# Three engine programs as loop bodies that run once, and a down projection in 512-column products

## The chip, the cores and the metric

The kernel runs on one core of a Trainium2 chip. The time is device microseconds (us) of one execution. The span is the time from the first to the last instruction in the profile of one execution; the time of an execution is a little longer than its span, and both are given below.

## The reference

One decode step of a gated mix of an attention block and a gated feed-forward block, both on the same four rows `x` (4 x 512, bf16).

```python
g = sigmoid((x * gate_w).sum(-1, keepdims=True))
# a: 32 query heads over 8 key/value heads, the last W = 4096 of 16384 positions
q = (x @ wq)                       # 4 x 4096
p = softmax(q . k / sqrt(128))     # per head, over 4096 positions
a = (p . v) @ wo                   # wo is 4096 x 512
# b: gated feed-forward with a relu gate
gate, up = x @ W_gate, x @ W_up    # 512 x 1792 each
b = (gate * (gate > 0) * up) @ W_down     # W_down is 1792 x 512
return g * a + (1 - g) * b         # 4 x 512
```

The window of keys and values is 4 batches x 8 heads x 4096 positions x 128 values, 33.5 MB each in bf16; with the weights some 81 MB have to be read.

## The kernel before

The work is cut into eight sets `s` (`NSET`), each one batch and four of its eight key/value heads. For each set one 4 MB transfer brings the keys into `Ksb[:, s % 2]` (`load_k`, line 217) and one the values into `Vsb[:, s % 2]` (`load_v`, line 221). Both buffers are double; `load_k(s)` waits until the scores of set `s - 2` have been made, `load_v(s)` until the value products of set `s - 2` are done. All bulk transfers are issued by SyncE (SP) in one written order: `wq`, keys and values in turn, `W_gate`, `W_up` (into the key buffer), the last values, `W_down` (into the value buffer), and `wo` in five pieces at `WO_CUTS` (lines 235 to 244), of which the last two (`WOL`) are halves over columns. ScalarE (ACT) issues two small loads of `x` and `gate_w` first of all (lines 224 and 225).

For each set, TensorE (PE) transposes the keys in eight fills of eight 128 x 128 transposes (`kt`, line 352), VectorE (DVE) and ACT copy the fills back (lines 359 and 357), PE makes the scores in two pairs (`scores`, line 373), DVE adds a mask and takes the maximum (line 383), a small product and a DVE operation spread the maximum (lines 390 and 395), ACT takes the exponent (line 403), DVE transposes the probabilities (line 413), PE multiplies by the values (`values`, line 421) and ACT copies the result (line 430). The set's maximum, exponent and value products are written one set later than its scores.

A small class `Program` collects the operations of each engine in lists, with named events between them; `emit` writes an engine's list as straight code with semaphore waits. For PE alone the list is cut at `turn_edge` marks: a head, four turns of two sets each as one hardware loop (`Fori`, lines 130 to 134, with a drain and semaphore decrements at its end), and a tail written straight behind the loop (line 136). The programs of DVE, ACT, GpSimd (POOL) and SP have no loop.

The tail holds the last set's maximum, exponent and value products, `combine(0)` and `combine(1)` (lines 440 to 451: the quotient by the row sums, rearranged into `oq`), `gateup` (line 457: `x` with `W_gate` and `W_up`; ACT takes the relu, DVE the product, transposes it and scales it by `1 - g` into `hT`, line 470), and the output products (`product`, line 503). These add `W_down` and `wo` into one accumulator `AB` for two halves of 256 output columns: half `u` uses the PE columns from `32 * u` on (`tile_position`), so that its result lies in partitions `32 * u` to `32 * u + 3`. There are 28 products for `W_down` (14 row blocks x 2 halves) and 64 for `wo`. DVE and ACT copy one half each into `outr` (lines 517 and 518), SP stores it (line 539), all engines meet at the end of the block (line 534), and SP waits for the store (line 556).

Of the kernel before, what the change touches and what calls it, by code (L numbers as in the profile page):

```python
# [1 line left out]

# [4 lines left out]
BF16 = mybir.dt.bfloat16  # L7
ACTF = mybir.ActivationFunctionType
ALU = mybir.AluOpType
# [10 lines left out]
NSET = 8  # L20
NFT = FF // 128
# [12 lines left out]
class Program:  # L34
# [81 lines left out]
            out.append((name is not None, tuple(here)))  # L116
        return out

    def emit(self, engine, eng, sems):
        ops = self.ops[engine]  # L120
        if engine != "pe":
            self.emit_list(eng, sems, engine, ops, {}, {})
            return
        t = self.turns
        self.emit_list(eng, sems, engine, ops[:t[0]], {}, {})
        first = self.signature(ops[t[0]:t[1]], {})
        for k in range(1, len(t) - 1):
            shift = {s: k * n for s, n in self.lowered.items() if s not in self.shared}
            assert self.signature(ops[t[k]:t[k + 1]], shift) == first, k
        with eng.Fori(0, len(t) - 1):  # L130
            self.emit_list(eng, sems, engine, ops[t[0]:t[1]], {}, {})
            eng.drain()
            for s, n in self.lowered.items():
                eng.sem_inc(sems[s], -n)
        shift = {s: (len(t) - 1) * n for s, n in self.lowered.items() if s not in self.shared}
        self.emit_list(eng, sems, engine, ops[t[-1]:], shift, {})


def bass_gated_mix__sliding_block_cached__glu_gated_reglu__decode_kernel(
# [13 lines left out]
    with ExitStack() as ctx:  # L153
        def sb(name, shape, dt):
            return ctx.enter_context(nc.sbuf_tensor(name, shape, dt))
# [16 lines left out]
        xsb = sb("xsb", [5, 512], BF16)  # L172
# [3 lines left out]
        gsb = sb("gsb", [128, 8], FP32)  # L176
# [12 lines left out]
        hrelu = sb("hrelu", [128, FQ], FP32)  # L189
        hrow = sb("hrow", [128, FQ], FP32)  # L190
        hcol = sb("hcol", [128, FQ], FP32)
        hT = sb("hT", [128, NFT * 4], BF16)
        outr = sb("outr", [4, 512], BF16)
        TRT = ctx.enter_context(nc.psum_tensor("TRT", [128, 2048], FP32))
        SCT = ctx.enter_context(nc.psum_tensor("SCT", [128, 1024], FP32))
        OB = ctx.enter_context(nc.psum_tensor("OB", [128, 512], FP32))
# [5 lines left out]
        Wd = Vsb[:, 0, 0:NFT * 512].rearrange("p (i w) -> p i w", w=512)  # L202
# [3 lines left out]
        P = Program()  # L206
# [45 lines left out]
        P.op("pool", lambda e: e.memset(xw[:, :], 0.0), ("XW0",))  # L252
        P.op("pool", lambda e: e.memset(mx[:, 1, :], 0.0))
        P.op("pool", lambda e: e.memset(pT[:, 1, :], 0.0))
        P.op("pool", lambda e: e.memset(xT[:, :, :].rearrange("p t r -> p (t r)"), 0.0))
        P.op("pool", lambda e: e.memset(qW[:, :, :, :].rearrange("p s h w -> p (s h w)"), 0.0), ("QZ",))
        P.op("pool", lambda e: e.memset(m4[:, :], -NEG), ("M4Z",))
# [40 lines left out]
        for t in range(4):  # L298
            P.op("pe", lambda e, t=t: e.matmul(FB[:, 32:36], gwB[:, t * 128:(t + 1) * 128], xT[:, t, 0:4],
                                               start=(t == 0), stop=(t == 3)),  # L300
# [5 lines left out]
        for t in range(4):  # L306
            for half in range(2):
                for g in range(4):
# [3 lines left out]
                        start=(t == 0), stop=(t == 3), tile_position=(0, 32 * g)),  # L312
# [140 lines left out]
        def gateup():  # L453
            for t in range(4):
                for which, W in ((0, Wg), (1, Wu)):
                    for g in range(4):
                        P.op("pe", lambda e, which=which, W=W, t=t, g=g: e.matmul(
                            TRT[32 * g:32 * g + 32, 512 * which:512 * which + FQ], xT[:, t, :], W[:, t, FQ * g:FQ * g + FQ],
                            start=(t == 0), stop=(t == 3), tile_position=(0, 32 * g)),
                            ("GU", which) if (t == 3 and g == 3) else None,  # L460
                            [("WG",), ("WU",)] + fills[-NTR:])
            G0 = TRT[:, 0:FQ]
            G1 = TRT[:, 512:512 + FQ]
            P.op("act", lambda e: e.activation(hrelu[:, :], G0, ACTF.Relu),
                 ("H0",), [("GU", 0)])
            P.op("dve", lambda e: e.tensor_tensor(
                hrow[:, :].rearrange("p (i c) -> p c i", i=NFT), G1.rearrange("p (c i) -> p c i", i=NFT),
                hrelu[:, :].rearrange("p (c i) -> p c i", i=NFT), ALU.mult), ("H1",), [("H0",), ("GU", 1)])
            P.op("dve", lambda e: e.transpose(hcol[:, :], hrow[:, :]), ("H2",), [("H1",)])
            P.op("dve", lambda e: e.tensor_tensor(  # L470
                hT[:, :].rearrange("p (i b) -> p i b", b=4),
                hcol[:, :].rearrange("p (i b) -> p i b", b=32)[:, :, 0:4],
                gsb[:, 4:8].rearrange("p (o b) -> p o b", o=1).to_broadcast([128, NFT, 4]), ALU.mult),
                ("H",), [("H2",), ("G",)], sem="vd")


# [17 lines left out]
        turn(NSET - 1)  # L494
        combine(0)
        gateup()
        values(NSET - 1)
        combine(1)
        AB = SCT[:, 0:512]
        oq3 = oq[:, :].rearrange("p (b i) -> p b i", b=4)  # L500

        def product(stat, mov, u, start, stop, name, waits):
            P.op("pe", lambda e: e.matmul(AB[32 * u:32 * u + 4, 0:256], stat, mov[:, 256 * u:256 * u + 256],  # L503
                                          start=start, stop=stop, tile_position=(0, 32 * u)), name, waits)

        for i in range(NFT):
            for u in range(2):
                product(hT[:, 4 * i:4 * i + 4], Wd[:, i, :], u, i == 0, False, None,
                        [("WD",), ("H",), ("SCC", NSET - 1, 1)])
        for k in range(len(WO_CUTS) - 1):  # L510
            for i in range(WO_CUTS[k], WO_CUTS[k + 1]):
                for u in range(2):
                    product(oq3[:, :, i], Wo3[:, i, :], u, False, False, None, [("WO", k), ("OQ", 0), ("OQ", 1)])
        for u in range(2):
            for i in range(WO_CUTS[-1], 32):
                product(oq3[:, :, i], Wo3[:, i, :], u, False, i == 31, ("ACC", u) if i == 31 else None, [("WOL", u)])
        P.op("dve", lambda e: e.tensor_copy(outr[:, 0:256], AB[0:4, 0:256]), ("FIN", 0), [("ACC", 0)], sem="fin")
        P.op("act", lambda e: e.copy(outr[:, 256:512], AB[32:36, 0:256]), ("FIN", 1), [("ACC", 1)], sem="fin")  # L518

        per = {}  # L520
        for s, ev in (("vd", ("SCC", 1, 1)), ("va", ("OSB", 0))):
            after = ("SCC", 3, 1) if s == "vd" else ("OSB", 2)
            eng = {"vd": "dve", "va": "act"}[s]
# [8 lines left out]
        sems = {name: ctx.enter_context(nc.semaphore(name)) for name in names}  # L532
        nc.sync.dma_start(Vsb[:, 1, :], A_wq.rearrange("(p t) w -> p (t w)", p=128)).then_inc(sems["V1"], 16)  # L533
        with nc.Block() as block:
            @block.sync
            def _(e):
                P.emit("sp", e, sems)
                e.wait_ge(sems["fin"], 2)
                e.dma_start(out.rearrange("b o d -> (b o) d"), outr[:, :]).then_inc(sems["done"], 16)

            @block.gpsimd
            def _(e):
                P.emit("pool", e, sems)

            @block.tensor
            def _(e):
                P.emit("pe", e, sems)

            @block.vector
            def _(e):  # L550
                P.emit("dve", e, sems)

            @block.scalar
            def _(e):
                P.emit("act", e, sems)
        nc.sync.wait_ge(sems["done"], 16)


# [26 lines left out]
```

## Time and profile before

| | |
|---|---|
| three runs, median | 196.53 us (196.35 to 196.71) |
| profiled execution, its own time | 196.16 us |
| its span | 194.9 us |
| busy: PE, PE weight loads, DVE, ACT, POOL | 129.2, 101.0, 73.8, 66.5, 11.7 us |
| read from HBM | 81.01 MB, 416 GB/s over the span |

The busy times overlap: no engine is busy for more than two thirds of the span. PE and its weight loads (PEld) are one engine, and a matmul's end is modelled, so a busy PE is not PE at its peak. The rows "DMA queue, kind" give the packets of each queue, their bytes in MB, and the time that they took as a share of 16 DMA engines over the stretch that is asked for. Queue 1 carries what SP issues, queue 10 what ACT issues, and the kind "instruction" marks packets that carry instructions to the engines.

### The profile page before, as it was taken

To read this page: it belongs to the slowest core of one execution; us is meant where nothing else is said; L and a number is where in the kernel's file an instruction comes from. 1 tells how busy PE (TensorE), PEld (TensorE's weight loads), DVE (VectorE), ACT (ScalarE), POOL (GpSimd) and SP (SyncE) were. 2 spreads that over 40 slices of the span, in tenths; PEclk is the share of its full clock that TensorE was granted. 3 is DMA by queue.
4 is the path that set the end of the run, shared out by engine and by line. 5 is a ranking of instruction groups with operands and counts; after the bars stand their busy time and mean duration, and the time that the engine had idled before them with its cause. 6 is when DMAs were issued, how large, how long until landed. Compare 5 with 4: busy or idle time off the path is not lost.

```text
span 194.9 us, 3496 instructions
## 1 busy us (share of the span) xinstructions
PE 129.2 (66%) x1578; PEld 101.0 (52%) x1578; DVE 73.8 (38%) x95; ACT 66.5 (34%) x77; POOL 11.7 (6%) x43
## 2 busy tenths in 40 slices
PE   0137398788769649872887099649972987713964
PEld 0113396576556439651765097439651865503742
DVE  0200045259239323930682029324920492180000
ACT  2005025565255452435342424433435252510000
POOL 8820000000000000000000000000000000000000
PEclk9999999999999996999999859996999699995799
DMA  6999999999999999999999999999999999998992
GB/s 216 431 430 437 430 430 427 437 440 430 437 440 430 437 430 437 430 430 437 432 437 425 430 437 430 430 437 430 430 430 430 430 390 427 475 430 382 424 403 82
DMA packets 3881, 81.11 MB, mean 416 GB/s; under 512 B 409, under 2 KB 930, under 8 KB 1058
## 3 DMA queue, kind: packets, MB, share of 16 engines
q1 hardware_dynamic: 3864, 81.01, 97.3%
q8 instruction: 5, 0.08, 0.2%
q14 instruction: 2, 0.02, 0.0%
q10 hardware_dynamic: 10, 0.01, 0.0%
HBM read 81.01 MB, written 0.00 MB: 416 GB/s over the span
## 4 chain that ended last, share of the span: by engine, by line
DMA 59%; PE 21%; DVE 14%; ACT 3%; issue 1%; SPq 1%
DMA Ksb<-in_A_k_cache_dram 47%; PE TRT L352 15%; DMA Wbig<-in_A_wo_dram 12%; DVE Ksb L359 6%; DVE pT L413 5%; PE SCT L373 3%; DVE sc L383 3%; ACT Ksb L357 3%; PE OB L421 2%; PE SCT L503 1%; SPq L240 0%; PE FB L390 0%; SPq L533 0%; ACT outr L518 0%; SPq L235 0%
## 5 line engine op out<-in xcount | busy, mean ns | idle before, releaser
L352 PE MATMUL TRT<-identw,Ksb 128*128 128x128 f32 x512 | 75.1, 306 | 25.4 <-DMA Ksb<-in_A_k_cache_dram 17.5
L352 PEld LDWEIGHTS TRT<-identw,Ksb 128*128 128x128 f32 x512 | 65.9, 158 | 35.8 <-DMA Ksb<-in_A_k_cache_dram 18.8
L357 ACT COPY Ksb<-TRT 128x1024 f32<-128x1024 f32 x40 | 40.5, 1012 | 58.4 <-PE TRT L352 58.2
L359 DVE COPY Ksb<-TRT 128x1024 f32<-128x1024 f32 x24 | 29.4, 1223 | 40.1 <-PE TRT L352 40.1
L421 PE MATMUL OB<-Vsb,pT 128*32 128x256 bf16 x576 | 19.0, 288 | 7.5 <-DMA Vsb<-in_A_v_cache_dram 7.5
L373 PE MATMUL SCT<-Ksb,qS 128*32 128x512 bf16 x256 | 16.9, 381 | 8.8 <-ACT Ksb L357 8.8
L421 PEld LDWEIGHTS OB<-Vsb,pT 128*32 128x32 bf16 x576 | 16.4, 101 | 10.4 <-issue 7.9
L383 DVE CUSTOM_DVE_ANT_0 sc<-SCT,mask,mx 128x1024 bf16<-128x1024 f32 x8 | 10.3, 1284 | 26.9 <-PE SCT L373 26.9
L403 ACT ACTIVATE sc<-sc,negmax 128x2048 bf16<-128x2048 bf16 x8 | 16.0, 2002 | 10.7 <-DVE negmax L395 10.7
L413 DVE STREAM_TRANSPOSE pT<-sc 128x2048 bf16<-128x2048 bf16 x8 | 18.4, 2302 | 2.2 <-ACT sc L403 2.2
L430 ACT COPY osb<-OB 128x256 f32<-128x256 f32 x8 | 3.0, 372 | 31.1 <-PE OB L421 31.1
L373 PEld LDWEIGHTS SCT<-Ksb,qS 128*32 128x32 bf16 x256 | 5.2, 94 | 15.7 <-ACT Ksb L357 11.6
L383 DVE CUSTOM_DVE_ANT_0 sc<-SCT,mask 128x1024 bf16<-128x1024 f32 x8 | 9.8, 1225 | 2.2 <-PE SCT L373 2.2
L340 POOL COPY qS<-qW 128x64 bf16<-128x64 bf16 x8 | 1.8, 238 | 113.3 <-PE SCT L373 105.2
L390 PE MATMUL FB<-identw,mx 128*128 128x128 f32 x18 | 4.7, 343 | 5.7 <-issue 5.7
L395 DVE CUSTOM_DVE_ANT_0 mrow<-FB,qmask 128x128 f32<-128x128 f32 x8 | 2.3, 292 | 12.8 <-PE FB L390 12.8
L390 PEld LDWEIGHTS FB<-identw,mx 128*128 128x128 f32 x18 | 2.9, 200 | 7.6 <-issue 7.6
L292 PE MATMUL FB<-identw,xw 5*128 5x5 f32 x4 | 0.6, 262 | 8.5 <-POOL m L267 8.5
L503 PE MATMUL SCT<-Wbig,oq 128*4 128x256 bf16 x64 | 4.3, 273 | 2.6 <-DMA Wbig<-in_A_wo_dram 2.6
L310 PE MATMUL SCT<-Vsb,xT 128*32 128x512 bf16 x32 | 3.6, 631 | 2.8 <-DMA Vsb<-in_A_wq_dram 2.8
L292 PEld LDWEIGHTS FB<-identw,xw 5*128 5x128 f32 x4 | 0.6, 207 | 8.5 <-DVE xw L286 8.5
L503 PEld LDWEIGHTS SCT<-Wbig,oq 128*4 128x4 bf16 x64 | 2.7, 87 | 4.2 <-DMA Wbig<-in_A_wo_dram 3.6
(61 smaller groups left out, 42.7 us busy)
## 6 DMA issues: line engine op xcount, KB each, us to landing
Ksb<-in_A_k_cache_dram SPq DMA_DIRECT2D x8, 4096.0 KB, 24.2
Vsb<-in_A_v_cache_dram SPq DMA_DIRECT2D x8, 4096.0 KB, 32.2
Vsb<-in_A_wq_dram SPq DMA_DIRECT2D x1, 4096.0 KB, 12.3
Wbig<-in_A_wo_dram SPq DMA_DIRECT2D x1, 2048.0 KB, 21.5
Ksb<-in_B_W_gate_dram SPq DMA_DIRECT2D x1, 1792.0 KB, 19.7
Ksb<-in_B_W_up_dram SPq DMA_DIRECT2D x1, 1792.0 KB, 23.6
Vsb<-in_B_W_down_dram SPq DMA_DIRECT2D x1, 1792.0 KB, 17.0
Wbig<-in_A_wo_dram SPq DMA_DIRECT2D x1, 1280.0 KB, 24.1
```

What stands on the lines that cost most here:

```text
L310: P.op("pe", lambda e, half=half, t=t, g=g, col=col: e.matmul(SCT[32 * g:32 * g + 32, 512 * half:512 * half + 512], xT[:, t, :], Wq3[:, t, ...
L352: P.op("pe", lambda e, bk=bk, cc=cc, c=c: e.transpose(bk[:, cc * 128:(cc + 1) * 128], Kw[:, s % 2, c * 128:(c + 1) * 128], identw[:, :]), ...
L357: P.op("act", lambda e: e.copy(dst, bk), ("KTC", s, i), [("KT", s, i)], sem="va")
L359: P.op("dve", lambda e: e.tensor_copy(dst, bk), ("KTC", s, i), [("KT", s, i)], sem="vd")
L373: P.op("pe", lambda e, a=a, o=o, hb=hb, bank=bank: e.matmul(SCT[32 * a:32 * a + 32, 512 * hb:512 * hb + 512], qS[:, s % 2, o, :], k4[:, 16 ...
L383: P.op("dve", lambda e: e.tensor_tensor_reduce(sc[:, s % 2, pair * 1024:(pair + 1) * 1024], SCT[:, :], mask[:, :], 1.0, mx[:, s % 2, 0:1] ...
L390: P.op("pe", lambda e: e.matmul(FB[:, 384:512], mx[:, par, 1:2].to_broadcast([128, 128]), identw[:, :], start=True, stop=True), ("MT", s), ...
L403: P.op("act", lambda e: e.activation(sc[:, par, :], sc[:, par, :], ACTF.Exp, bias=negmax[:, par:par + 1], scale=SCALE, accum_out=rowsum[:, ...
L413: P.op("dve", lambda e: e.transpose(pT[:, par, :], sc[:, par, :]), ("PTT", s), [("EXP", s), ("PV", s - 2) if s >= 1 else None], sem="vd")
L421: P.op("pe", lambda e, g=g, blk=blk: e.matmul(OB[32 * g:32 * g + 32, 0:256], pT[:, par, 32 * blk:32 * blk + 32], Vsb[:, par, 256 * blk:256 ...
L430: P.op("act", lambda e: e.copy(osb[:, s, :], OB[:, 0:256]), ("OSB", s), [("PV", s)], sem="va")
L503: P.op("pe", lambda e: e.matmul(AB[32 * u:32 * u + 4, 0:256], stat, mov[:, 256 * u:256 * u + 256], start=start, stop=stop, tile_position=( ...
```

## The change

ACT's and DVE's whole programs and the tail of PE's program are each put into a block that ends in a compare-and-branch. A register is set to 0 ahead of the block, 1 is added at its end, and the branch back to the block's top is taken while the register is below 1, so never; the block runs once. At the block's top a branch hint is placed that names this branch (the compiled program marks it "likely taken"). PE's loop over the four turns is left as it is, and POOL and SP get no such block.

The products with `W_down` go over all 512 columns at once. Their stationary operand is widened to 36 columns, of which columns 0 to 3 and 32 to 35 hold the same four rows of `h` and the 28 between hold zeros; so 14 products write all 512 columns into both partition groups, where 28 wrote 256 columns each. `hT` grows from 56 to 504 columns for it, is zeroed once by POOL, and DVE's line that fills it writes two copies. The `wo` products of half 1 now write columns 256 to 511 of `AB`, where they wrote 0 to 255. The result is copied into `xsb`, which held `x`, instead of `outr`, which goes.

```diff
+    @contextmanager
+    def once(self, nc, engine, eng):
+        top, end = engine + "_once", engine + "_once_end"
+        reg = eng.alloc_register(engine + "_turns")
+        eng.reg_mov(reg, 0)
+        eng.br(top)
+        with nc.body(top, valid_engines=bass.OrderedEngineSet([eng.engine])):
+            place = eng.mark_branch_hint_location()
+            yield
+            eng.reg_add(reg, reg, 1)
+            eng.br_lt(reg, 1, on_true=top, on_false=end).branch_hint(place)
+        nc.switch_bb(end)
+
-    def emit(self, engine, eng, sems):
+    def emit(self, nc, engine, eng, sems):
         ops = self.ops[engine]
+        if engine in ("dve", "act"):
+            with self.once(nc, engine, eng):
+                self.emit_list(eng, sems, engine, ops, {}, {})
+            return
...
-        self.emit_list(eng, sems, engine, ops[t[-1]:], shift, {})
+        with self.once(nc, engine, eng):
+            self.emit_list(eng, sems, engine, ops[t[-1]:], shift, {})
...
-        hT = sb("hT", [128, NFT * 4], BF16)
-        outr = sb("outr", [4, 512], BF16)
+        hT = sb("hT", [128, 36 * NFT], BF16)
...
+        P.op("pool", lambda e: e.memset(hT[:, :], 0.0))
...
-                hT[:, :].rearrange("p (i b) -> p i b", b=4),
-                hcol[:, :].rearrange("p (i b) -> p i b", b=32)[:, :, 0:4],
-                gsb[:, 4:8].rearrange("p (o b) -> p o b", o=1).to_broadcast([128, NFT, 4]), ALU.mult),
+                hT[:, :].rearrange("p (k b i) -> p k i b", k=9, b=4)[:, 0:9:8],
+                hcol[:, :].rearrange("p (k i b) -> p k i b", k=1, b=32)[:, :, :, 0:4].to_broadcast([128, 2, NFT, 4]),
+                gsb[:, 4:8].rearrange("p (k o b) -> p k o b", k=1, o=1).to_broadcast([128, 2, NFT, 4]), ALU.mult),
...
+        def wide(stat, mov, start, waits):
+            P.op("pe", lambda e: e.matmul(AB[0:36, :], stat, mov, start=start, stop=False), None, waits)
...
-            P.op("pe", lambda e: e.matmul(AB[32 * u:32 * u + 4, 0:256], stat, mov[:, 256 * u:256 * u + 256],
+            P.op("pe", lambda e: e.matmul(AB[32 * u:32 * u + 4, 256 * u:256 * u + 256], stat, mov[:, 256 * u:256 * u + 256],
...
-            for u in range(2):
-                product(hT[:, 4 * i:4 * i + 4], Wd[:, i, :], u, i == 0, False, None,
-                        [("WD",), ("H",), ("SCC", NSET - 1, 1)])
+            wide(hT[:, i:i + 35 * NFT + 1:NFT], Wd[:, i, :], i == 0, [("WD",), ("H",), ("SCC", NSET - 1, 1)])
...
-        P.op("dve", lambda e: e.tensor_copy(outr[:, 0:256], AB[0:4, 0:256]), ("FIN", 0), [("ACC", 0)], sem="fin")
-        P.op("act", lambda e: e.copy(outr[:, 256:512], AB[32:36, 0:256]), ("FIN", 1), [("ACC", 1)], sem="fin")
+        P.op("dve", lambda e: e.tensor_copy(xsb[0:4, 0:256], AB[0:4, 0:256]), ("FIN", 0), [("ACC", 0)], sem="fin")
+        P.op("act", lambda e: e.copy(xsb[0:4, 256:512], AB[32:36, 256:512]), ("FIN", 1), [("ACC", 1)], sem="fin")
```

More of the change, by code (lines that the diff above doesn't have):

```diff
@@ L1 @@
-from contextlib import ExitStack
+from contextlib import ExitStack, contextmanager
 import concourse.bass as bass
@@ L536, in _ @@
             def _(e):
-                P.emit("sp", e, sems)
+                P.emit(nc, "sp", e, sems)
                 e.wait_ge(sems["fin"], 2)
-                e.dma_start(out.rearrange("b o d -> (b o) d"), outr[:, :]).then_inc(sems["done"], 16)
+                e.dma_start(out.rearrange("b o d -> (b o) d"), xsb[0:4, :]).then_inc(sems["done"], 16)
             @block.gpsimd
             def _(e):
-                P.emit("pool", e, sems)
+                P.emit(nc, "pool", e, sems)
             @block.tensor
             def _(e):
-                P.emit("pe", e, sems)
+                P.emit(nc, "pe", e, sems)
             @block.vector
             def _(e):
-                P.emit("dve", e, sems)
+                P.emit(nc, "dve", e, sems)
             @block.scalar
             def _(e):
-                P.emit("act", e, sems)
+                P.emit(nc, "act", e, sems)
         nc.sync.wait_ge(sems["done"], 16)
```

## Prediction

> **What bounds the kernel now.** I read the page's DMA queues first, then the end of the chain that ended last.
>
> ```profile
> span 194.9 us, 3496 instructions
> DMA  6999999999999999999999999999999999998992
> q1 hardware_dynamic: 3864, 81.01, 97.3%
> q8 instruction: 5, 0.08, 0.2%
> q14 instruction: 2, 0.02, 0.0%
> ...
> 166.62 24.15 DMA Wbig<-in_A_wo_dram
> ...
> 190.81 2.38 PE SCT L503 x32
> ...
> 193.22 0.36 ACT outr L518
> ```
>
> The DMA engines are busy in all slices but the first and the last two; SP's own queue takes 97.3% of them. The chain (start, length) ends in the transfer of `wo`, then the last products, one copy, and the store up to 194.9. So two things can move the end: the time at which the last of `wo` lands, and what follows it.
>
> Seven packets carry instructions. They use the same 16 engines as the data. Where they lie, by the DMA view over the stretches 31 to 32.5, 54 to 56, 93 to 95, 182 to 183.7 and 191.8 to 193 us, in this order:
>
> ```profile
> q8 instruction: 1, 0.02, 4.3%
> q8 instruction: 1, 0.02, 3.2%
> q14 instruction: 1, 0.01, 1.0%
> q8 instruction: 1, 0.02, 3.9%
> q8 instruction: 1, 0.02, 4.8%
> ```
>
> The two not shown are a q8 packet at 42 to 43.5 and a q14 packet at 104 to 105.5. Taking a packet as sent by one engine, its time is share x 16 x stretch: 0.043 x 16 x 1.5 = 1.03 us, then 1.02, 0.32, 1.06 and 0.92 us. Whose are they? The busy counts (PE, PEld, DVE, ACT, POOL in this order) between the first three q8 packets:
>
> ```profile
> 31.86:42.59 10.73, 8.61 (x129) 7.13 (x127) 4.97 (x8) 6.13 (x7) 0.24 (x1) 1.00 0.97 415
> 42.59:54.88 12.29, 9.13 (x138) 6.65 (x136) 7.07 (x7) 4.68 (x6) 0.24 (x1) 1.00 1.03 444
> ```
>
> PE runs 129 + 127 = 256 and 138 + 136 = 274 instructions; no other engine runs more than 8 or so. So q8 is PE's code, one packet for each 256 instructions or thereabouts: three in the first turn, none in turns 2 to 4 (the same code again), two in the tail. The two small ones, far apart, belong by exclusion to DVE and ACT, whose straight programs run in that time. The Trainium skill's page "Runtime: NRT & Kernel Launch", section "Instruction fetch mechanics", says that code comes in blocks of 16 KiB, 256 instructions, the next block while the current one runs; the q8 rows agree, the q14 rows have half blocks.
>
> What do these packets cost? The share of busy DMA engines (the last but one column) as the transfers run out:
>
> ```profile
> 190.40:190.80 0.40, 0.00 (x0) 0.00 (x0) 0.00 (x0) 0.00 (x0) 0.00 (x0) 1.00 0.77 254
> 190.80:191.20 0.40, 0.39 (x8) 0.33 (x10) 0.00 (x0) 0.00 (x0) 0.00 (x0) 1.00 0.42 151
> 191.20:191.50 0.30, 0.30 (x10) 0.24 (x8) 0.00 (x0) 0.00 (x0) 0.00 (x0) 1.00 0.36 123
> 191.50:191.90 0.40, 0.40 (x12) 0.24 (x6) 0.00 (x0) 0.00 (x0) 0.00 (x0) 1.00 0.29 86
> 191.90:192.10 0.20, 0.20 (x6) 0.03 (x4) 0.00 (x0) 0.00 (x0) 0.00 (x0) 1.00 0.54 156
> 192.10:192.40 0.30, 0.30 (x7) 0.24 (x8) 0.00 (x0) 0.00 (x0) 0.00 (x0) 1.00 0.12 34
> ```
>
> About seven engines (0.42 x 16) still work when the others are through, five after 191.5. They are late by up to 1.5 us, the length of one 16 KB packet and a little; five packets on a single engine would make one engine late by 5 us. So I read: each packet fell on an engine of its own, and the four 16 KB packets ahead of 191 us made four engines late by about the same. The work in these rows, 0.31 + 0.17 + 0.11 + 0.12 + 0.11 + 0.04 = 0.84 us of all 16, less 0.92 / 16 = 0.06 for the last packet, would end at 190.40 + 0.78 = 191.2 if spread evenly; it ends at some 192.4. So 1.2 us is all that no code at all could give.
>
> **The change part by part.** *Hints.* What a hint does no row here shows. At most, code is no longer brought from behind the branch: both q14 packets and the two in the tail go (four of seven). At least, nothing goes; below that, each hint brings its target again (three packets more). The three q8 packets of PE's first turn stay in every case, since that loop is untouched, and their three engines are late by as much as the fourth. The end of `wo` is the latest engine's, so removing the 182 us packet gives what it is later than the others: between 0 and its 1.06 us, and by the reading above nearly 0. The q14 packets (0.32 us) delay engines that are not the last: 0. The 191.9 us packet starts when at most five engines still carry data; unless it is on one of those (5 in 16, and then late by at most what data is left there), 0. Bounds of this edit: -1.2 and +1.06 us; I take 0, the row of six dwindling shares being the nearest.
>
> *Entry of the blocks.* A register move and a hint on each engine.
>
> ```profile
> PE FB L390 <- issue: 5.7, 4, 1.5
> 4.11 0.52 POOL L256 MEMSET qW<- 128x512 bf16 x1
> 8.00 0.44 DVE L286 COPY xw<-xsb 5x512 bf16<-5x512 bf16 x1 [8.00 <-POOL S L262]
> 9.79 0.16 DVE L297 COPY xT<-FB 128x16 bf16<-128x16 bf16 x1
> 13.12 3.60 PE L310 MATMUL SCT<-Vsb,xT 128*32 128x512 bf16 x32 [2.84 <-DMA Vsb<-in_A_wq_dram]
> 178.59 3.60 PE L421 MATMUL OB<-Vsb,pT 128*32 128x256 bf16 x64 [7.50 <-DMA Vsb<-in_A_v_cache_dram]
> ```
>
> PE's turn edge, with drain, six semaphore decrements, an addition and a branch, costs at most 1.5 us (first row: total, times, longest). An entry is bounded by 0 and that; I take 0.2, as it has two of nine instructions. On ACT it delays the loads of `x` and `gate_w`, behind which DVE's first operation, the transposes of `x` and the projection with `wq` are queued. `xT` is there at 9.95 and the projection waits for `wq` until 13.12: 3.2 us of cover. On PE, the wait for the last values (7.50 us) hides it. POOL's added memset (504 columns, so about the 0.52 us of `qW`'s 512) and DVE's second copy lie in the same two covers. All 0.
>
> *W_down.* 28 products over 256 columns, in pairs on two column groups, become 14 over 512 columns, unpaired.
>
> ```profile
> 184.62 1.69 PE L503 MATMUL SCT<-Vsb,hT 128*4 128x256 bf16 x28
> 187.70 1.92 PE L503 MATMUL SCT<-Wbig,oq 128*4 128x256 bf16 x32 [1.39 <-DMA Wbig<-in_A_wo_dram]
> 190.81 2.37 PE L503 MATMUL SCT<-Wbig,oq 128*4 128x256 bf16 x32 [1.19 <-DMA Wbig<-in_A_wo_dram]
> L373 PE MATMUL SCT<-Ksb,qS 128*32 128x512 bf16 x256 | 16.9, 381 | 8.8 <-ACT Ksb L357 8.8
> ```
>
> If pairs did not overlap before, nothing changes (1.69); if they did fully, twice 1.69 = 3.38. The score products (four 512-column ones side by side) give 16.9 / 64 = 0.264 per pass, 14 x 0.264 = 3.70. I take 3.38: the end moves from 186.31 to 188.00 (188.32 at 3.70). The first `wo` products then end at 189.92 (190.24) instead of 189.62, and the next piece of `wo` is awaited until 190.81. Cover left: 0.89 (0.57) us. Cost 0; at half the clock it would be 6.76 us, a rival below.
>
> *Exit.* An addition and a branch not taken, on three engines, then the meeting at the block's end.
>
> ```profile
> 192.93 0.41 DVE L517 CAST outr<-SCT 4x256 bf16<-4x256 f32 x1 [7.49 <-PE SCT L503]
> 193.60 0.35 SPq L539 DMA_DIRECT2D out_dram<-outr  x1
> SPq L556 <- DMA out_dram<-outr: 0.5, 1, 0.5
> ```
>
> PE ends at 193.18, DVE at 193.34, ACT at 193.58 by the chain; SP issues the store until 193.95 and after the meeting still waits 0.5 us for it. So PE may be late by 193.95 - 193.18 + 0.5 = 1.27 us, DVE by 1.11, ACT by 0.87. Two instructions, bounded by 0 and the turn edge's 1.5, taken at 0.2: hidden. The Trainium skill's page "Advanced Engine Details and Errata", section "Control Flow Timing", gives a compare-and-branch about 108 ns; by it the sum would be the same.
>
> Sum: 0 + 0 + 0 + 0. The span stays 194.9 and the profiled execution's 196.16 us with it. The median of the runs shown is 196.53, 0.37 above that execution; I forecast the median: **196.5 us**. About 0.2% (0.39 us) is what a measurement of this kernel can tell from no change.
>
> **The rivals.** *The exit stalls (slower).* If a hint sends the fetch back to the loop's top, the block behind the branch isn't there when the branch falls through. The last q8 packet was called near the end: after 191.9 only the 12 products of the rows from 192.07 on are left. The tail becomes 28 instructions shorter and some four longer, so PE's exit comes close to that very border. For it: the trace never shows a block running without a packet ahead of it. Against it: PE may read ahead while its products wait, and fetch early. Price: the store's issue to the end, 194.9 - 193.95 = 0.95 us for a small transfer, plus 0.92 for the packet: 1.87 us from 193.18 is 195.05, past the cover's end (193.95 + 0.5 = 194.45) by 0.60; for ACT with a half block 193.58 + 0.95 + 0.33 = 194.86, by 0.41. A second stall in what runs after the block would add 1.87. So +0.4 to +2.5, taken as +0.9: 197.4. It decides from a stall of 1.27 us on PE or 0.87 on ACT. The Runtime page's rule, in the section named, is that a branch outside the sequential stream waits for its block, and that straight code is to be preferred; by that rule the result is this rival.
>
> *The removed packet was the last (faster).* If the engine of the 182 us packet ends `wo` alone, or two packets share an engine in most executions, up to 1.06 us goes, and at most 1.2: 195.3 to 196.1, taken as 195.6. For it: packets are late in the right size. Against it: five engines, not one, are still busy after 191.5.
>
> *W_down at half clock (slower).*
>
> ```profile
> 37.15 1.92 PE L421 MATMUL OB<-Vsb,pT 128*32 128x256 bf16 x64
> ```
>
> The last set's 64 value products took 3.60 us where this earlier set's took 1.92, at half the clock. With `W_down` so: 184.62 + 6.76 = 191.4, then the 64 `wo` products, 1.92 + 2.37 = 4.3 us: 195.7 instead of 193.2, and 199.0 in all. Against it: the clock column (after POOL's) reads 1.00 from 190.4 on, and at 184.62 the products already run at the full pace of the rows above; it decides only if the half clock lasts longer than before.
>
> *The hint does nothing*: 196.5, part of the forecast.
>
> **How the numbers follow.** Forecast (with the idle hint) 0.47, its own range 196.1 to 196.9; exit stall or extra packets 0.31; half clock 0.02; removed packet 0.20. So faster 0.20, same 0.47, slower 0.33. The range reaches from 195.7 (a little beyond the middle of the faster case) to 197.9 (most of the stall).
>
> **What would show it.** Right: q8 packets at 31 to 56 us as before, none at 93 to 105, the shares after 190.8 unchanged, `W_down` ending before 188.4, the last product at 193.2. Wrong: PE's first product behind the wait for values later than 178.6; the last piece of `wo` landing over 0.4 us earlier or later; the wait of SP at the block's end longer than its wait for the store; a longer time with the same span, which would be a stall outside it.

## The result: 1.3% slower, by a stall of TensorE at its exit

| | before | changed |
|---|---|---|
| median | 196.44 us (196.14 to 196.71, 4 runs) | 199.02 us (4 runs) |
| ratio | | 1.0128, interval 1.0112 to 1.0144 |
| profiled execution | 196.16 us | 198.27 us |
| its span | 194.9 us | 196.6 us |
| beyond the span | 1.26 us | 1.67 us |

Of the four runs of the changed kernel three took 198.27, 198.88 and 199.16 us; the fourth, at 648.01 us, was disturbed by something that no record explains and is in the median, but not in the ratio. The profiled execution is the shortest of the three; the spans of the other two are 197.2 and 197.5 us, so more of the loss lies within the span there than in the views that follow.

The profiled execution is 2.1 us longer: 1.7 us within the span, 0.4 us beyond it. First the page's head and two of its queue rows, then the end of the timeline (start, length, engine, line; SPq and PEq stand for SyncE's and TensorE's instruction streams where they issue or wait; in the changed kernel `W_down`'s products are line 522, `wo`'s line 525, the store line 559):

```profile
span 196.6 us, 3481 instructions
...
q8 instruction: 4, 0.07, 0.1%
q14 instruction: 1, 0.01, 0.0%
```

```profile
167.54 0.48 PE L410 MATMUL FB<-identw,mx 128*128 128x128 f32 x2 [1.52 <-issue]
...
184.46 2.97 PE L522 MATMUL SCT<-Vsb,hT 128*36 128x512 bf16 x13
...
187.83 1.92 PE L525 MATMUL SCT<-Wbig,oq 128*4 128x256 bf16 x32 [0.41 <-DMA Wbig<-in_A_wo_dram]
...
191.02 2.28 PE L525 MATMUL SCT<-Wbig,oq 128*4 128x256 bf16 x32 [1.27 <-DMA Wbig<-in_A_wo_dram]
...
193.72 0.35 SPq L559 DMA_DIRECT2D out_dram<-xsb  x1
```

The `wo` products end at 193.30, 0.12 us later than before, and the store is issued 0.12 us later. Up to here that is all the loss. What follows is in the view of SP's own waits, one row of before and the one of the changed kernel for the same place, the meeting of the engines at the block's end:

```profile
SPq L534 <- PEq L534: 0.2, 1, 0.2
```

```profile
SPq L554 <- PEq L554: 2.2, 1, 2.2
```

SP now waits 2.2 us for PE, where it waited 0.2; and its wait for the store, 0.5 us before, is no longer in the view, since the store had long landed. That is the loss in the span: 2.0 more, 0.5 of it covered by the store, 0.12 from the later `wo`: 1.6 of the 1.7 us. In the trace's records PE's branch begins at 193.01 and the next instruction of its stream, the drain, at 196.30: 3.29 us, of which the last products fill the first 0.3.

The DMA view shows what moved in that time. There is no q8 packet from 176 to 190 us, where before had one at 182; there is one in the stretch 193.5 to 195.5:

```profile
q8 instruction: 1, 0.02, 2.8%
```

0.028 x 16 x 2 = 0.90 us of one engine: one 16 KB block of code, fetched while the 4 KB store of the result is all that moves besides. It starts at 193.96, 0.95 us after the branch, and PE goes on 1.45 us after it ended. That PE waits for this block is a reading so far; the experiments bear on it.

And the packets that the hints removed? The share of busy DMA engines (last column but one) after 191.5, as in the prediction's rows:

```profile
191.50:191.90 0.40, 0.40 (x13) 0.33 (x9) 0.00 (x0) 0.00 (x0) 0.00 (x0) 1.00 0.19 60
...
192.10:192.40 0.30, 0.30 (x8) 0.13 (x6) 0.00 (x0) 0.00 (x0) 0.00 (x0) 1.00 0.16 46
```

After 191.5 there are 0.19 x 16 = 3 late engines instead of 0.29 x 16 = 4.6. So the fetch of 182 us did make an engine late, and that engine is no longer late; but the three of PE's first turn still are, and `wo` lands no earlier. The trace's sixteen arrivals of the last transfer, taken as one from each engine, say the same. Before, ten lie between 191.04 and 191.41 us, two at 192.0 and four between 192.50 and 192.75: two and four are also the numbers of 8 KB and of 16 KB packets ahead of them. In the changed kernel twelve lie before 191.5, one at 191.84 and three between 192.69 and 192.87, with one and three such packets ahead.

The packet of 191.9 us is gone too, but it is missing as well in the two runs below that have the wide products and no hint, so the shorter tail removes it. The two q14 packets of before are gone as well; the one on the page is another, at 131 us, whose engine I cannot name from the views.

### The profile page after: what moved, and what is told of

It is laid out like the page before. It is cut to its first block, busy times and chain, and to the rows that moved or that the text cites. A ratio compares the mean times of both kernels' runs of the same rounds, so it can differ in the third digit from the quotient of the medians.

```text
span 196.6 us, 3481 instructions
## 1 busy us (share of the span) xinstructions
PE 130.6 (66%) x1564; PEld 102.0 (52%) x1564; DVE 74.2 (38%) x95; ACT 66.5 (34%) x77; POOL 12.1 (6%) x44
## 4 chain that ended last, share of the span: by engine, by line
DMA 59%; PE 21%; DVE 14%; ACT 3%; issue 1%; SPq 1%
DMA Ksb<-in_A_k_cache_dram 47%; PE TRT L372 14%; DMA Wbig<-in_A_wo_dram 12%; DVE Ksb L379 6%; DVE pT L433 5%; PE SCT L393 3%; DVE sc L403 3%; ACT Ksb L377 3%; PE OB L441 2%; PE SCT L525 1%; SPq L259 0%; PE FB L410 0%; SPq L553 0%; ACT xsb L538 0%; SPq L254 0%
```

## Experiments

The theory, H: with PE's hint, the fetch goes to the loop's top when PE enters the block of code that holds the hinted branch, and the block behind it is missing at the exit. Its rivals: the branch itself stalls (L); ACT's and DVE's hints make the loss (D); the shorter straight tail does (B). A run's "before" are 25 runs on the same chip, with medians of 196.18 to 196.21 us.

H is a theory in its first half: no packet shows a fetch of the loop's top. What the runs can show is whether the packet of the next block comes or not.

**Without the hints.**

```diff
-            place = eng.mark_branch_hint_location()
...
-            eng.br_lt(reg, 1, on_true=top, on_false=end).branch_hint(place)
+            eng.br_lt(reg, 1, on_true=top, on_false=end)
```

> The changed kernel with its three blocks, its branches and its wide W_down products, but without the three hints. Theory H (PE's hint keeps the block behind the branch from being fetched ahead): the q8 packet at about 182 us is back, SP's wait for PE at the block's end falls from 2.2 us to some 0.2 to 0.4, the two q14 packets are back, the span is 194.7 to 195.2 and the time 196.2 to 196.8. Rival L (the branch at the end stalls by itself, hint or not): span 196.6 or longer, time 198.3 to 199.2, SP's wait for PE still about 2.2 us.

Measured: 196.26 us, ratio 1.000 (0.9991 to 1.001), span 195.1. From the page, then from the DMA view over 176 to 190 us, then from SP's waits:

```profile
q14 instruction: 2, 0.02, 0.0%
```

```profile
q8 instruction: 1, 0.02, 0.5%
```

```profile
SPq L553 <- PEq L553: 0.2, 1, 0.2
```

The packet of 182 us is back, both q14 packets are back, and the stall is gone with blocks, branches and `W_down` as in the changed kernel. L falls: the hints make the loss, and with them the packet of the next block is missing.

**PE's block and hint alone; ACT's and DVE's alone; neither.** The three have the wide `W_down` products.

```diff
 # PE alone
-        if engine in ("dve", "act"):
-            with self.once(nc, engine, eng):
-                self.emit_list(eng, sems, engine, ops, {}, {})
-            return
 # ACT and DVE alone
-        with self.once(nc, engine, eng):
-            self.emit_list(eng, sems, engine, ops[t[-1]:], shift, {})
+        self.emit_list(eng, sems, engine, ops[t[-1]:], shift, {})
 # neither: both edits
```

> The changed kernel with the block and the hint on PE's tail alone; ACT's and DVE's programs are straight. Theory H: the stall at PE's exit is here in full, SP waits 2.2 us for PE, span 196.4 to 196.9; if the 0.4 us by which the time beyond the span had grown belong to ACT and DVE, the time beyond the span is back at 1.2 us and the time 197.6 to 198.2; if they belong to PE, it stays at 1.7 and the time at 198.1 to 198.9. Rival D (ACT's and DVE's hints make the loss): time 196.2 to 196.8.

> The changed kernel with blocks and hints on ACT and DVE alone; PE's tail is straight, with the wide W_down products. Theory H: no stall at PE's end, q8 packet at about 182 us there, SP's wait for PE 0.2 to 0.4 us, span 194.7 to 195.2; time 196.2 to 196.8 if what is beyond the span belongs to PE, 0.4 us more if it belongs to ACT and DVE. Rival D: time 198.3 to 199.2.

> The kernel before with the wide W_down products alone; no blocks, no hints. Reading of the prediction: W_down ends before 188.4, the next piece of wo is awaited as before, span 194.7 to 195.2, time 196.2 to 196.8, the same as before. Rival B (the shorter straight tail by itself brings PE's end to a border between code blocks and stalls there): SP's wait for PE over 1 us and the time over 197.3.

Measured: PE alone 198.93 us (196.98 to 199.59), ratio 1.011 (1.005 to 1.017); ACT and DVE alone 196.56, ratio 1.0024 (1.0011 to 1.0037); neither 196.17, ratio 1.0001 (0.9991 to 1.0011). So B falls, the wide products cost nothing, and PE's hint makes most of the loss, though one of its four executions took only 196.98. But the loss is not where I expected it. PE alone, from its page, then from SP's waits:

```profile
span 195.1 us, 3473 instructions
...
q8 instruction: 3, 0.05, 0.1%
```

```profile
SPq L550 <- PEq L550: 0.2, 1, 0.2
```

Here the span is as before, and PE is on time for the meeting. The profiled execution took 199.46 us all the same, 4.4 us beyond its span instead of 1.26, the packet of 182 us is missing, and one of 16 KB starts at 196.31, behind the span's last instruction. By my count in the compiled program, which no view shows, the code behind PE's branch stands four places earlier in this kernel than in the changed one (fewer labels for ACT's and DVE's blocks). A border of code blocks within those few places would explain it: in the changed kernel it would lie before PE's drain, here behind PE's part in the meeting, and the same stall would fall into what runs after the block. The border itself is inferred.

**The place of the exit.** If so, moving the exit beyond the border must take the stall away. One run goes back to 28 `W_down` products with all three hints, which puts 28 instructions in front of the exit; one keeps PE's hint alone and the wide products and puts 32 instructions of no use there.

```diff
 # all hints, narrow
...
-            wide(hT[:, i:i + 35 * NFT + 1:NFT], Wd[:, i, :], i == 0, [("WD",), ("H",), ("SCC", NSET - 1, 1)])
+            for u in range(2):
+                product(hT[:, 4 * i:4 * i + 4], Wd[:, i, :], u, i == 0, False, None,
+                        [("WD",), ("H",), ("SCC", NSET - 1, 1)])
...
 # PE's hint alone, padded: behind gateup()
+        for _ in range(16):
+            P.op("pe", lambda e: e.matmul(SCT[:, 512:516], ident[:, :], ident[:, 0:4], start=True, stop=True))
```

> The changed kernel with all three blocks and hints, but with the W_down products of the kernel before (28 over 256 columns). PE's program ends 28 instructions later in it, so that its exit lies beyond the border of code blocks near the end. Theory H with the border: the block that holds the exit was fetched at about 182 us, PE doesn't stall at the exit, SP's wait for PE is 0.2 to 0.4 us and the span 194.7 to 195.2; time 196.3 to 196.9, the loss that ACT's and DVE's hints alone had shown (ratio 1.0024). Rival (PE's hint stalls wherever the exit lies): span 196.4 or more or 2 to 4 us more beyond the span, time 198 to 199.6.

> The kernel with the block and the hint on PE's tail alone and the wide W_down products, and with 16 small products of four columns (32 instructions) added in the wait for the last values; their result is not used. The only thing that matters in it is where the exit lies: 32 instructions later, beyond the border. Theory H with the border: q8 packet at about 182 us, no stall, time 196.0 to 196.6 against 198.93 without the 32 instructions, so more instructions make it some 2.5 us faster. Rival (the hint stalls wherever the exit lies): 198.4 to 199.6. Rival (W_down matters): unchanged from 198.9 too, since W_down is the same.

Measured: 196.33 us, ratio 1.0012 (0.9999 to 1.0026), and 196.14 us, ratio 0.9997 (0.9987 to 1.0006). In both SP waits 0.2 us for PE, and the narrow one has its packet of 182 us. The padded kernel, DMA view over 176 to 190 us:

```profile
q8 instruction: 1, 0.02, 0.5%
```

32 instructions more make it 2.8 us faster in the median (196.14 against 198.93), and the packet of 182 us is back. It is the place of the exit that decides, not `W_down` as such. In the changed kernel the shorter program, 28 instructions fewer, is what brought the exit to the place where it stalls. One of the eleven padded executions, the profiled one, took 197.79 us with a span of 195.0; the single hints below bear on that.

**DVE's hint alone; ACT's hint alone.**

```diff
-        if engine in ("dve", "act"):
+        if engine == "dve":      # and: engine == "act"
```

> The changed kernel with the block and the hint on DVE alone; PE's and ACT's programs are straight, the W_down products wide. The loss with ACT and DVE was 0.24%, all beyond the span. If it is DVE's: 196.4 to 197.0 with some runs near 197.1, the q14 packet at about 94 or 105 us gone, the other there. If it is ACT's: 196.0 to 196.4. If each has a part: 196.3 to 196.5.

> The changed kernel with the block and the hint on ACT alone; PE's and DVE's programs are straight, the W_down products wide. DVE alone had the ratio 1.0013, both together 1.0024. If each has a part: 196.3 to 196.5 with a ratio of 1.001 and some runs near 197.1. If the loss is DVE's: 196.0 to 196.3 and no run above 196.6.

Measured: 196.29 us, ratio 1.0013 (0.9998 to 1.0028), and 196.22, ratio 1.0012 (0.9999 to 1.0025). No change lies within the interval of each; together they gave 1.0024. Of ten runs each, three, and one, are near 197.3 and the others mostly as before, with the spans unchanged at 195.0. So about 1 us is lost in some executions, beyond the span. The traces point to a place. The profiled execution of DVE alone is one of the long ones (197.26), and its DMA view over 195 to 199 us has one q8 packet of 16 KB, behind the span; so has that of the padded kernel (197.79). The profiled executions of between 196.0 and 196.5 us of the other kernels, ACT alone and ACT with DVE among them, have none there. So a block of PE's code, fetched behind the span, goes with the longer time, even where PE has no hint. Why it is fetched in some executions only stays open.

These two runs also name the small packets: the DMA view of DVE alone has no q14 packet from 104 to 108 us, that of ACT alone none from 93 to 97. The packet near 105 us is DVE's and the one near 94 us is ACT's.

**Where packets of code fall.** The forecast rested on each packet having an engine of its own. So I added code to the kernel before: on POOL, while it is idle, 896 one-column memsets; as a control the same bytes in 112 memsets; and on PE, in the wait for the last values, 128 instructions, so that its last packet comes earlier.

```diff
 # behind each set's copy into qS; the control: 16 memsets of 8 columns a set
+            for k in range(max(128 * s - 128, 0), 128 * s):
+                P.op("pool", lambda e, k=k: e.memset(spare[:, k:k + 1], 0.0))
...
 # PE: behind gateup()
+        for _ in range(64):
+            P.op("pe", lambda e: e.matmul(SCT[:, 512:516], ident[:, :], ident[:, 0:4], start=True, stop=True))
```

> The kernel before, with 128 added one-column memsets on POOL behind each set's small copy but the first (896 in all, into a buffer that nothing reads), while POOL is idle: seven more packets of 8 KB of code, some 0.32 us of one DMA engine each. Reading of the prediction (each packet delays an engine of its own, and only the latest engine counts): the end of wo moves by 0 to 0.35 us, time 196.0 to 196.7. Rival (all packets of one queue fall on one engine): that engine is 7 x 0.32 = 2.3 us late, time 197.2 to 198.5.

> The control of the run with 896 small memsets on POOL, which was 2.8 us slower: the same bytes of the same buffer are set in 112 memsets of eight columns, so POOL's program is longer by one code block instead of seven. If the packets of code made the loss: one packet more, at most some 0.6 us on one engine, and the end of wo on the other engines as before: 196.0 to 196.8. If POOL's writes themselves slowed the transfers: still 198 or more.

> The kernel before, with 64 small products of four columns (128 instructions) added to PE's tail in the wait for the last values; their result is not used. PE then passes the last border of code blocks some 128 instructions earlier, so that the q8 packet of 191.9 us comes at 185 to 188 us, with data still to come on all engines: a fifth 16 KB packet that can delay data. Reading of the prediction (PE's packets fall on an engine each, and only the latest engine counts): 196.0 to 196.7. Rival (it falls on an engine that had a packet): that engine lands 1.3 us later, 197.2 to 197.8.

Measured: 199.00 us, ratio 1.0143 (1.0126 to 1.016); control 196.19, ratio 1.000 (0.999 to 1.0009); PE 196.19, ratio 0.9998 (0.9989 to 1.0008). For POOL my reading was wrong and the rival right in kind: it had 197.2 to 198.5 us, from 0.32 us a packet, and the loss is larger. The q14 row of its page, the engines' share from 192.8 us on, and the last products in the timeline (line 506 in this kernel):

```profile
q14 instruction: 9, 0.07, 0.1%
```

```profile
192.80:194.00 1.20, 0.08 (x2) 0.00 (x0) 0.00 (x0) 0.00 (x0) 0.00 (x0) 1.00 0.05 22
```

```profile
194.01 2.38 PE L506 MATMUL SCT<-Wbig,oq 128*4 128x256 bf16 x32 [1.13 <-DMA Wbig<-in_A_wo_dram]
```

Two of the nine are those that before has too, at 96 and 108 us. From 192.8 to 194.0 the share is 0.05, and 0.05 x 16 is 0.8: one engine, alone, still brings its part of `wo`, and PE waits for it until 194.01 where it had gone on at 190.81. By the arrivals of the last transfer that engine is 3.3 us behind the next latest (195.96 against 192.71), and some 4.7 behind the middle of the ten punctual ones. The others are as late as before: four at 192.5 to 192.7, one at 192.04. So the seven packets added no second late engine. That all seven, perhaps with one of ACT's or DVE's, fell on this one is the reading that fits; it makes 0.6 to 0.7 us each. No view names a packet's engine. The control sets as many bytes by POOL and loses nothing, so the bytes are not the cause; what is left is the 784 instructions more and the six packets that they bring. For PE the reading held: the added instructions bring a packet at 187.7 us (stretch 186 to 190), and in the stretch 191.5 to 191.9 six engines (0.38 x 16) are late instead of 4.6, at no cost; by the arrivals five engines, not four, land at 192.5 or later.

```profile
q8 instruction: 1, 0.02, 1.7%
```

```profile
191.50:191.90 0.40, 0.40 (x12) 0.34 (x8) 0.00 (x0) 0.00 (x0) 0.00 (x0) 1.00 0.38 117
```

No run beat the kernel before. None was expected to: all that removes packets in the tail leaves the three of PE's first turn, and their engines land as late as the fourth.

## Why the prediction was wrong, point by point

*What bounds the kernel*: right. The removed packets were worth nothing, for the reason given (three late engines stay). The narrow kernel with all hints had no q14 packet in its span and the same time (196.33 us).

*Each packet has an engine of its own*: right for PE's four or five and for the two of ACT and DVE, by the arrivals; wrong as a rule, since POOL's seven made one engine late by some 4.7 us and no other.

*What the hint does*: bounded at "four of seven packets go" as the most, and so it was: both q14 packets and the one of 182 us went with the hints, the one of 191.9 us with the shorter tail, and a block came at the exit instead.

*Entry*: right. PE's wait at the tail's start grew from 1.30 to 1.52 us (0.2 was taken), ACT's first load is issued at 0.95 instead of 0.80; both covered.

*W_down*: right. From 184.18 to 187.43, 3.25 us against 3.38, and the wait for `wo` remains.

*Exit*: this is the step that failed. I took 0.2 us for "an addition and a branch not taken" and called it hidden under a cover of 1.27 us for PE, so 0 in the sum; it took 3.29 and the span grew by 1.7. (For DVE and ACT 0.2 was right: their drains start 0.12 and 0.10 us after their branches.) The row used, PE's turn edge with at most 1.5 us, is of a branch whose code is there: turns 2 to 4 bring no packet. The rival "the exit stalls" named the mechanism, the border, the 28 instructions and the point from which it decides, and had 0.31 against 0.47. So the case named as the likelier was the wrong one. What I held against it, that PE would read ahead while its products wait, is refuted: the addition in front of the branch starts at 192.91, with PE's last wait for `wo`.

*The rival's price* was too small as well: 1.87 us for a fetch (0.95 for a small transfer and 0.92 for the packet) against 3.29. Those two terms measured 0.95 and 0.89; missing are the 1.45 us from the packet's end to PE's next instruction. It gave 0.60 in the span, where 1.7 was measured. Another 0.4 us came on top beyond the span; ACT's and DVE's hints are candidates for it, and no run shows it.

The Trainium skill's page "Runtime: NRT & Kernel Launch", section "Instruction fetch mechanics", says that a taken branch to a block that isn't loaded waits for its fetch and that prefetch is purely sequential. The direction was right and the case another: here a branch that is not taken waits for 3.29 us, and with the hint the next block's packet is missing, so the fetch did not just go on in sequence; the run without hints has the same branch, the packet and a wait of 0.2 us at the meeting.

## What to carry to other kernels

Code is fetched over the same DMA engines as the data, so in a kernel bound by transfers look at the rows of the kind "instruction": here the latest engine decided what a packet costs, and removing one of four equally late ones was worth nothing. A hint that a branch will be taken is a promise about the fetch: on PE's branch, which falls through, the next block of code did not come ahead, and the price came due in the exit or behind the span. Where such a price depends on the place of an instruction in its block, count instructions before believing that fewer are better.

## What the runs showed of the hardware

- A code block that PE had not got cost it 3.29 us with the DMA engines almost idle (one profiled execution): 0.95 until the packet starts, 0.89 for its 16 KB, 1.45 until PE goes on.
- A packet of code made its engine later than the packet is long: in the kernel before, by the arrivals, about 1.5 us behind the punctual engines for 1.0 us (16 KB), about 0.8 for 0.32 us (8 KB).
- PE's four or five packets made four or five DMA engines late; seven added packets of POOL made one engine late, by some 4.7 us.
- The loss of PE's hint showed as a wait in the span (changed kernel) or wholly beyond it (PE's hint alone: span 195.1, time 199.46). A span that is unchanged does not say that the time is.
